# First batch of a fused cross-covariance attention and max-out feed-forward kernel: q norms as column sums on TensorE, products with the weights in landing order, third weight behind the first hidden products

## Chip, cores, metric

One core of a Trainium2 chip. The metric is the device time of one execution in microseconds. Kernel before: 574.05 us (three runs, 574.01 to 574.26). In lines and tables PE is TensorE (PEld its weight loads), DVE VectorE, ACT ScalarE, POOL GpSimd and SP SyncE. To evacuate is to copy a result from PSUM to SBUF.

## The reference

```python
qn = q / (norm(q, axis=1) + 1e-06)           # q, k, v: 4 x 6144 x 256; norms over the 6144 tokens
kn = k / (norm(k, axis=1) + 1e-06)
s  = kn.T @ qn / tau                          # 256 x 256 for each batch
a  = softmax(s, axis=-1)
x  = v @ a
h  = max(x @ w1, x @ w2, x @ w3)              # d_ff 768
out = h @ w_out
```

Because a is only 256 x 256, the kernel multiplies it into the weights first (the "A^T W products": the tiles `ew_ps`, evacuated to `aw`), so that each chunk of 512 tokens costs 36 products of 128x512 (`h_ps`) and 24 of 128x256 (`o_ps`). The 768 columns of each weight are taken in slices of 256. Warming products are products whose results nobody uses; they fill TensorE's wait for the softmax.

## The kernel before

The parts that matter (cuts marked):

```python
    def gram(b):
        ...                                             # kk: the k norms, while k is arriving
        for tp in range(NG // 2):                       # 24 steps, while q is arriving
            for j in range(CC):
                PE.matmul(ps[j][:, 0:C], lhsT=qt[:, tsl, jsl], rhs=kt[:, tsl, :], ...)          # Gram
                PE.matmul(ps[j][:, C:C + P], lhsT=qt[:, tsl, jsl], rhs=qt[:, tsl, jsl], ...)    # q by q: its diagonal is |q|^2
        ...
    def softmax_t(ps, rkb):
        for j in range(CC):
            DVE.tensor_tensor_reduce(out=scr, in0=ps[j][:, C:C + P], in1=ident, ..., accum_out=n2q[:, j:j + 1])
        ACT.activation(out=lnq, in_=n2q, func=AF.Ln)
        ACT.activation(out=rq, in_=lnq, func=AF.Exp, scale=-0.5, bias=neg_ln_tau)
        return exp_t(scaled([ps[j][:, 0:C] for j in range(CC)], rkb), rq)      # et: the softmax, two halves j

    def aw_first(et, aw):                               # first 256 columns of the three weights
        products(0, (0, 1)); sums(0); sums(1)
        DVE.reciprocal(out=rinv, in_=rs_ps[:, 0:CC])
        products(1, (0, 1))
        for j in range(CC):
            products(j, (2,))
        ...                                             # six evacuations, ACT and DVE in turn

    first = gram(0); six warming products; softmax_t; v_transpose_pe(0); aw_first
    v_transpose(1); hold_loads(1)                       # a guard: waits for the second V's transpose
    POOL.dma_start(out=wo_sb, in_=moe_w_out...)         # the output weight
    load_v(2); load_v(3)
    ...                                                 # then 48 chunks: h blocks and output products
```

## Time and profile before

| what | value | where it is read |
|---|---|---|
| time | 574.05 us | median of three runs |
| TensorE busy | 553.9 us, 97% of a 572.1 us span | page, part 1 |
| last piece of q in | 33.63 us | end of the wait for q in the chain |
| first h product | 37.52 us | timeline |
| products with the second slice of the weights start (end of the first h block) | 38.81 us | timeline |
| output products start | 50.63 us | timeline |

The prediction, quoted below, shows the page's chain. Here is the stretch after the last piece of q, from the timeline of the kernel before (columns: start, duration, engine, line, operation, count, and in brackets the idle time ahead of it with what ended it):

```profile
34.87 0.20 ACT L286 ACTIVATE lnq<-n2q 128x2 f32<-128x2 f32 x1 [6.00 <-DVE n2q L282]
35.34 0.91 ACT L275 ACTIVATE et<-e_in,rq 128x256 bf16<-128x256 f32 x2
36.47 0.60 ACT L377 ACTIVATE vt_sb<-vt_ps 128x512 bf16<-128x512 bf16 x1 [0.23 <-DVE vt_sb L376]
36.70 0.17 DVE L341 RECIPROCAL rinv<-rs_ps 128x2 f32<-128x2 f32 x1 [0.27 <-PE rs_ps L329]
36.97 1.21 ACT L347 ACTIVATE aw_sb<-ew_ps,rinv 128x256 bf16<-128x256 f32 x3
36.98 1.27 DVE L349 TENSOR_SCALAR aw_sb<-ew_ps,rinv 128x256 bf16<-128x256 f32 x3
37.49 0.12 PEld L389 LDWEIGHTS <-aw_sb 128*128 128x128 bf16 x2 [0.21 <-ACT aw_sb L347]
38.81 0.38 PE L311 MATMUL ew_ps<-w_sb,et 128*128 128x256 bf16 x2
```

Read it as a relay: the norms (Ln at 34.87), the softmax (35.34), the reciprocal of its row sums (36.70), the evacuations on two engines (36.97), the first h weights (37.49), and the next slice of weights at 38.81. The line at 36.47 is ScalarE's copy of its half of the transposed V.

### The profile page before, as it was taken

What the parts mean: (1) busy time and instruction counts of PE and PEld (TensorE: products, weight loads), DVE (VectorE), ACT (ScalarE), POOL (GpSimd) and SP (SyncE); (2) the same over time, 40 slices, a digit from 0 to 9 for tenths busy, and PEclk for the clock granted to TensorE, in tenths of its full rate; (3) what the DMA queues carried; (4) which work ended last, traced back from release to release, by engine and by line L of the source; (5) the groups of instructions that cost most, each with busy time, mean ns of one, the idle gap of its engine ahead of it and who ended that gap; (6) DMA issues with size and microseconds to landing.
All of it is one profiled execution on the core that took longest, in us unless ns stands there. A gap on an engine that the chain in (4) does not pass through costs nothing.

```text
span 572.1 us, 9442 instructions
## 1 busy us (share of the span) xinstructions
PE 553.9 (97%) x3349; PEld 330.7 (58%) x3350; DVE 411.1 (72%) x647; ACT 309.1 (54%) x539; POOL 235.1 (41%) x240
## 2 busy tenths in 40 slices
PE   3799999999999999999999999999999999999997
PEld 2665555555755555555575555555575555555566
DVE  0048777877577777777768777777868778778775
ACT  1044567677454576776545467767645444444443
POOL 2443357776730078776560048777750000000000
PEclk9999999999999999999999999999999999999999
DMA  9998998884598168984179339885437323132112
GB/s 143 106 146 129 136 237 126 159 135 116 99 107 160 56 107 158 134 148 110 57 128 151 99 81 140 148 141 98 124 86 154 75 75 109 56 103 64 56 55 76
DMA packets 76960, 65.64 MB, mean 115 GB/s; under 512 B 52464, under 2 KB 62576, under 8 KB 76784
## 3 DMA queue, kind: packets, MB, share of 16 engines
q0 software_dynamic: 19072, 26.48, 38.7%
q1 hardware_dynamic: 57696, 38.41, 23.7%
q8 instruction: 26, 0.43, 0.3%
q14 instruction: 22, 0.18, 0.1%
q10 hardware_dynamic: 144, 0.13, 0.1%
HBM read 78.64 MB, written 25.17 MB: 181 GB/s over the span
## 4 chain that ended last, share of the span: by engine, by line
PE 93%; DMA 5%; POOL 0%; issue 0%; DVE 0%; POOLq 0%
PE h_ps L389 65%; PE o_ps L409 22%; DMA q_sb<-in_q_dram 5%; PE gram L260 3%; PE ew_ps L311 3%; POOL k_sb L99 0%; PE o_ps L434 0%; PE ew_ps L335 0%; PE warm_ps L469 0%; PE vt_ps L372 0%; PE gram L177 0%; PE n_ps L215 0%; DVE ht_sb L395 0%; DVE o_sb L461 0%; PE n_ps L217 0%
## 5 line engine op out<-in xcount | busy, mean ns | idle before, releaser
L389 PE MATMUL h_ps<-vt_sb,aw_sb 128*128 128x512 bf16 (+1 forms) x1764 | 406.7, 375 | 0.1
L389 PEld LDWEIGHTS <-aw_sb 128*128 128x128 bf16 x1764 | 171.8, 98 | 161.3 <-DVE aw_sb L317 2.0
L394 DVE TENSOR_TENSOR s_mx<-h_ps,s_mx 128x512 bf16<-128x512 f32 (+1 forms) x294 | 198.7, 676 | 87.1 <-ACT s_mx L393 86.8
L393 ACT ACTIVATE s_mx<-h_ps 128x512 bf16<-128x512 f32 (+1 forms) x294 | 172.4, 587 | 124.9 <-PE h_ps L389 124.0
L395 DVE TENSOR_TENSOR ht_sb<-h_ps,s_mx 128x512 bf16<-128x512 f32 (+1 forms) x294 | 200.2, 681 | 31.4 <-PE o_ps L409 0.5
L203 POOL TENSOR_TENSOR acc<-acc,sq 128x768 f32<-128x768 f32 x90 | 147.6, 1651 | 70.5 <-ACT sq L197 61.6
L409 PE MATMUL o_ps<-wo_sb,ht_sb 128*128 128x256 bf16 x1128 | 153.9, 273 | 0.0
L409 PEld LDWEIGHTS <-ht_sb 128*128 128x128 bf16 x1128 | 110.4, 98 | 52.0
L412 ACT ACTIVATE o_sb<-o_ps 128x512 f32<-128x512 f32 x94 | 56.1, 597 | 85.3 <-PE o_ps L409 85.3
L110 POOL DMA_DIRECT2D v_sb<-in_v_dram x48 | 27.5, 578 | 37.7 <-DMA vt_sb<-v_sb 35.5
L197 ACT ACTIVATE sq<-q_sb 128x768 bf16<-128x768 fp8e4 x48 | 40.5, 845 | 0.0
L197 ACT ACTIVATE sq<-k_sb 128x768 bf16<-128x768 fp8e4 x48 | 40.1, 835 | 0.0
L200 POOL CAST acc<-sq 128x768 f32<-128x768 bf16 x6 | 4.9, 823 | 68.7 <-ACT sq L197 68.7
L102 POOL DMA_DIRECT2D q_sb<-in_q_dram x33 | 18.4, 564 | 5.1 <-DMA v_sb<-in_v_dram 4.1
L165 PE MATMUL kk<-k_sb 128*128 128x256 fp8e4 x48 | 7.5, 338 | 11.9 <-DVE k_sb L151 6.3
L99 POOL DMA_DIRECT2D k_sb<-in_k_dram x29 | 16.1, 555 | 3.1 <-DMA v_sb<-in_v_dram 1.2
L260 PE MATMUL gram<-k_sb,q_sb 128*128 128x512 fp8e4 x144 | 16.8, 277 | 0.0
L260 PEld LDWEIGHTS <-q_sb 128*128 128x256 fp8e4 x144 | 15.9, 136 | 0.6
L314 ACT ACTIVATE aw_sb<-ew_ps,rinv 128x384 bf16<-128x384 f32 (+1 forms) x24 | 13.2, 555 | 5.5 <-PE ew_ps L311 4.7
L311 PE MATMUL ew_ps<-w_sb,et 128*128 128x384 bf16 (+1 forms) x96 | 15.6, 313 | 0.0
L177 PE MATMUL gram<-k_sb,q_sb 128*128 128x512 fp8e4 x48 | 11.4, 332 | 2.6 <-DMA q_sb<-in_q_dram 2.4
L165 PEld LDWEIGHTS <-k_sb 128*128 128x256 fp8e4 x48 | 6.4, 182 | 12.9 <-DMA k_sb<-in_k_dram 6.6
(67 smaller groups left out, 112.9 us busy)
## 6 DMA issues: line engine op xcount, KB each, us to landing
out_dram<-o_sb SPq DMA_DIRECT2D x41, 512.0 KB, 2.9
v_sb<-in_v_dram POOLq DMA_DIRECT2D x48, 256.0 KB, 4.2
k_sb<-in_k_dram POOLq DMA_DIRECT2D x24, 192.0 KB, 6.0
q_sb<-in_q_dram POOLq DMA_DIRECT2D x24, 192.0 KB, 7.6
out_dram<-o_sb SPq DMA_DIRECT2D x13, 256.0 KB, 2.0
k_sb<-in_k_dram POOLq DMA_DIRECT2D x5, 256.0 KB, 10.8
w_sb<-in_moe_w_dram POOLq DMA_DIRECT2D x9, 128.0 KB, 5.7
kf<-in_k_dram SPq DMA_DIRECT2D x1, 1024.0 KB, 4.8
```

Of the source, the lines that this page charges most:

```text
L102: POOL.dma_start(out=qk[b][0][:, g0:g0 + w, :], in_=q_r[b][:, g0:g0 + w, :])
L110: POOL.dma_start(out=t, in_=v_r[gi // NCH, gi % NCH])
L197: ACT.activation(out=sq, in_=src, func=AF.Square)
L203: POOL.tensor_tensor(out=acc, in0=acc, in1=sq, op=ALU.add)
L260: PE.matmul(g[:, j * C:(j + 1) * C], lhsT=qt[:, tsl, j * P:(j + 1) * P], rhs=kt[:, tsl, :], start=(tp == 0 and j == 0), stop=(tp == NG // ...
L311: PE.matmul(ew[:, :w], lhsT=et[:, j, ic * P:(ic + 1) * P], rhs=w_sb[m][:, j, fsl], start=(j == 0), stop=(j == CC - 1))
L389: PE.matmul(t.rearrange("p (t n) -> p t n", n=P), lhsT=aw[m][:, ic, fsl], rhs=vt[:, tsl, ic, :], start=(ic == 0), stop=(ic == CC - 1))
L393: ACT.activation(out=s_mx, in_=hp[0], func=AF.Copy)
L394: DVE.tensor_tensor(out=s_mx, in0=hp[1], in1=s_mx, op=ALU.max)
L395: DVE.tensor_tensor(out=ht, in0=hp[2], in1=s_mx, op=ALU.max)
L409: PE.matmul(st["ps"][:, half], lhsT=ht[:, fc, t * P:(t + 1) * P], rhs=wo_sb[:, fc, :], start=(fc == 0), stop=(fc == FC - 1))
L412: ACT.activation(out=st["o"][:, t - 1:t + 1, :].rearrange("p t d -> p (t d)"), in_=st["ps"], func=AF.Copy)
```

## The change

The intent: norms that need no DVE reduction behind the last piece of q; softmax row sums ahead of the products; and an h block that can start before the third weight has landed. The core of the diff (cut where marked):

```diff
-            for j in range(CC):
-                PE.matmul(ps[j][:, 0:C], ...)
-                PE.matmul(ps[j][:, C:C + P], lhsT=qt[:, tsl, jsl], rhs=qt[:, tsl, jsl], ...)
+        def squares(g0, w):                            # half of each piece of q on each engine
+            ACT.activation(out=a[:, 0:h, :], in_=ra, func=AF.Square)
+            DVE.tensor_tensor(out=d[:, 0:h, :], in0=rd, in1=rd, op=ALU.mult)
+        def columns(rows, first=False, last=False):    # |q|^2: squares by a column of ones
+            ... PE.matmul(nq[:, j:j + 1], lhsT=t[:, r, j * P:(j + 1) * P], rhs=ones_c, ...)
+        for i, w in enumerate(QW):                     # 8 8 8 8 4 4 4 2 2 groups
+            if rows:
+                columns(rows, first=(i == 1))          # of the piece before
+            ...                                        # Gram of this piece
+            rows = squares(g0, w)
+        columns(rows, last=True)
...
-        products(0, (0, 1))
+        weight(0)
         sums(0)
+        products(0, 0)
         sums(1)
         DVE.reciprocal(out=rinv, in_=rs_ps[:, 0:CC])
-        products(1, (0, 1))
+        products(1, 0)
+        weight(1)
         for j in range(CC):
-            products(j, (2,))
-        ...                                            # six evacuations in turn
+            products(j, 1)
+        for m in range(2):
+            evacuate(CC * m, ACT)
+            evacuate(CC * m + 1, DVE)
+        def third():                                   # called in the first h block, behind its first two products
+            weight(2)
+            for j in range(CC):
+                products(j, 2)
+            for ic in range(CC):
+                evacuate(2 * CC + ic, DVE)
...
+            if m == 0 and behind_first:
+                behind_first()
...
-    for i in range(6):
+    for i in range(2):                                 # warming products
```

The PE transposes of the first V are also split over two PSUM banks (six to DVE, two to ACT, instead of four and four).

More of the change, by code (lines that the diff above doesn't have):

```diff
@@ L75 @@
     sq_pool = ctx.enter_context(tc.tile_pool(name="sq", bufs=4))
+    sqq_pool = ctx.enter_context(tc.tile_pool(name="sqq", bufs=3))
     sm = ctx.enter_context(tc.tile_pool(name="sm", bufs=2))
@@ L118 @@
     SP.dma_start(out=kf, in_=k_r[0][:, 0:HEAD, :])
-    for load, widths in ((load_k, [8] * 5), (load_q, [8] * 4 + [4, 4, 4, 2, 2])):
+    QW = [8] * 4 + [4, 4, 4, 2, 2]
+    for load, widths in ((load_k, [8] * 5), (load_q, QW)):
         g0 = HEAD if load is load_k else 0
@@ L154, with gram_first @@
     neg_ln_tau = -math.log(float(tau)) if float(tau) != 1.0 else 0.0
-    def gram(b):
-        qt, kt = qk[b]
+    def gram_first():
+        qt, kt = qk[0]
         kk = htile("kk")
@@ L170, in gram @@
             DVE.tensor_tensor(out=dkm[:, jsl], in0=kk[:, jsl], in1=ident, op=ALU.mult)
-        ps = [xtile(f"gram{j}") for j in range(CC)]
-        for tp in range(NG // 2):
-            tsl = slice(2 * tp, 2 * tp + 2)
-            last = tp == NG // 2 - 1
-            for j in range(CC):
-                jsl = slice(j * P, (j + 1) * P)
-                PE.matmul(ps[j][:, 0:C], lhsT=qt[:, tsl, jsl], rhs=kt[:, tsl, :],
-                          start=(tp == 0), stop=last, perf_mode=DR, skip_group_check=True)
-                PE.matmul(ps[j][:, C:C + P], lhsT=qt[:, tsl, jsl], rhs=qt[:, tsl, jsl],
-                          start=False, stop=last, perf_mode=DR, skip_group_check=True)
-            if tp == 11:
+        g = xtile("gram")
+        nq = htile("nq")
+        def squares(g0, w):
+            h = w // 2
+            a = sqq_pool.tile([P, QW[0] // 2, C], BF16, name="sqa")
+            d = sqq_pool.tile([P, QW[0] // 2, C], BF16, name="sqd")
+            ra, rd = qt[:, g0:g0 + h, :], qt[:, g0 + h:g0 + w, :]
+            ACT.activation(out=a[:, 0:h, :], in_=ra, func=AF.Square)
+            DVE.tensor_tensor(out=d[:, 0:h, :], in0=rd, in1=rd, op=ALU.mult)
+            return [(t, r) for t in (a, d) for r in range(h)]
+        def columns(rows, first=False, last=False):
+            for n, (t, r) in enumerate(rows):
+                for j in range(CC):
+                    PE.matmul(nq[:, j:j + 1], lhsT=t[:, r, j * P:(j + 1) * P], rhs=ones_c,
+                              start=(first and n == 0 and j == 0), stop=(last and n == len(rows) - 1),
+                              skip_group_check=True)
+        g0 = 0
+        rows = None
+        for i, w in enumerate(QW):
+            if rows:
+                columns(rows, first=(i == 1))
+            for tp in range(g0 // 2, (g0 + w) // 2):
+                tsl = slice(2 * tp, 2 * tp + 2)
+                for j in range(CC):
+                    PE.matmul(g[:, j * C:(j + 1) * C], lhsT=qt[:, tsl, j * P:(j + 1) * P], rhs=kt[:, tsl, :],
+                              start=(tp == 0 and j == 0), stop=(tp == NG // 2 - 1), perf_mode=DR,
+                              skip_group_check=True)
+            rows = squares(g0, w)
+            g0 += w
+            if i == 2:
                 kb_ps = htile("kb_ps")
@@ L187, in gram @@
                 ACT.activation(out=rkb, in_=lnk, func=AF.Exp, scale=-0.5)
-        return ps, rkb
+        columns(rows, last=True)
+        return [g[:, j * C:(j + 1) * C] for j in range(CC)], rkb, nq[:, 0:CC]
     SQW = 3
@@ L276, in exp_t, with softmax_first @@
         return et
-    def softmax_t(ps, rkb):
-        n2q = sm.tile([P, CC], FP32, name="n2q")
-        scr = sm.tile([P, P], FP32, name="scr")
-        for j in range(CC):
-            DVE.tensor_tensor_reduce(out=scr, in0=ps[j][:, C:C + P], in1=ident, scale=1.0, scalar=0.0,
-                                     op0=ALU.mult, op1=ALU.add, accum_out=n2q[:, j:j + 1])
+    def softmax_first(gs, rkb, n2q):
         lnq = sm.tile([P, CC], FP32, name="lnq")
@@ L287, in softmax_t @@
         ACT.activation(out=rq, in_=lnq, func=AF.Exp, scale=-0.5, bias=neg_ln_tau)
-        return exp_t(scaled([ps[j][:, 0:C] for j in range(CC)], rkb), rq)
+        return exp_t(scaled(gs, rkb), rq)
     def alloc_aw():
@@ L324, in aw_first, with weight @@
         rs_ps = xtile("rs_ps")
-        parts = [(m, ic, htile("ew_ps")) for m in range(3) for ic in range(CC)]
+        parts = []
+        def weight(m):
+            parts.extend((m, ic, htile("ew_ps")) for ic in range(CC))
         def sums(j):
@@ L330, in sums, with products, evacuate @@
                           start=(ic == 0 and j == 0), stop=(j == CC - 1), skip_group_check=True)
-        def products(j, ms):
+        def products(j, of):
             for m, ic, ew in parts:
-                if m in ms:
+                if m == of:
                     PE.matmul(ew[:, :FT], lhsT=et[:, j, ic * P:(ic + 1) * P], rhs=w_sb[m][:, j, 0:FT],
                               start=(j == 0), stop=(j == CC - 1))
-        products(0, (0, 1))
+        def evacuate(n, engine):
+            m, ic, ew = parts[n]
+            dst, src, r = aw[m][:, ic, 0:FT], ew[:, :FT], rinv[:, ic:ic + 1]
+            if engine is ACT:
+                ACT.activation(out=dst, in_=src, func=AF.Copy, scale=r)
+            else:
+                DVE.tensor_scalar_mul(out=dst, in0=src, scalar1=r)
+        weight(0)
         sums(0)
+        products(0, 0)
         sums(1)
         DVE.reciprocal(out=rinv, in_=rs_ps[:, 0:CC])
-        products(1, (0, 1))
+        products(1, 0)
+        weight(1)
         for j in range(CC):
-            products(j, (2,))
-        for n, (m, ic, ew) in enumerate(parts):
-            if n % 2 == 0:
-                ACT.activation(out=aw[m][:, ic, 0:FT], in_=ew[:, :FT], func=AF.Copy, scale=rinv[:, ic:ic + 1])
-            else:
-                DVE.tensor_scalar_mul(out=aw[m][:, ic, 0:FT], in0=ew[:, :FT], scalar1=rinv[:, ic:ic + 1])
-        return rinv
+            products(j, 1)
[4 more added lines that the diff above has]
+            weight(2)
+            for j in range(CC):
+                products(j, 2)
+            for ic in range(CC):
+                evacuate(2 * CC + ic, DVE)
+        return rinv, third
     vts = {}
@@ L369, in v_transpose_pe, with h_block @@
         vt = vt_tile(gi)
-        vt_ps = xtile("vt_ps", cols=TPC * C, dtype=BF16)
-        for i in range(TPC * CC):
-            PE.matmul(vt_ps[:, i * P:(i + 1) * P], lhsT=v_sb[:, i * P:(i + 1) * P], rhs=ident,
-                      is_transpose=True, start=(i == 0), stop=(i == CC * TPC - 1))
-        half = TPC * CC // 2
-        ps = vt_ps.rearrange("p (i n) -> p i n", n=P)
-        DVE.tensor_copy(out=vt[:, half:, :], in_=ps[:, half:, :])
-        ACT.activation(out=vt[:, :half, :], in_=ps[:, :half, :], func=AF.Copy)
-    def h_block(gi, aw, fc, tsl=slice(0, TPC)):
+        n = TPC * CC
+        cut = 6
+        banks = [xtile("vt_ps", cols=TPC * C, dtype=BF16), ps_h.tile([P, TPC * C], BF16, tag="h", name="vt_ps2")]
+        for b, (lo, hi) in enumerate(((0, cut), (cut, n))):
+            for i in range(lo, hi):
+                PE.matmul(banks[b][:, i * P:(i + 1) * P], lhsT=v_sb[:, i * P:(i + 1) * P], rhs=ident,
+                          is_transpose=True, start=(i == lo), stop=(i == hi - 1))
+        pa, pb = (t.rearrange("p (i n) -> p i n", n=P) for t in banks)
+        DVE.tensor_copy(out=vt[:, 0:cut, :], in_=pa[:, 0:cut, :])
+        ACT.activation(out=vt[:, cut:n, :], in_=pb[:, cut:n, :], func=AF.Copy)
+    def h_block(gi, aw, fc, tsl=slice(0, TPC), behind_first=None):
         vt = vts[gi]
@@ L463, in last_chunk @@
         SP.dma_start(out=dst[:, HT + 1, :], in_=o_sb[:, HT + 1, :])
-    ps = gram(0)
+    first = gram_first()
     warm_ps = htile("warm_ps")
-    for i in range(6):
-        PE.matmul(warm_ps, lhsT=ident, rhs=warm, start=(i == 0), stop=(i == 5))
-    et = softmax_t(*ps)
+    for i in range(2):
+        PE.matmul(warm_ps, lhsT=ident, rhs=warm, start=(i == 0), stop=(i == 1))
+    et = softmax_first(*first)
     v_transpose_pe(0)
     aw = alloc_aw()
-    rinv = aw_first(et, aw)
+    rinv, third = aw_first(et, aw)
     v_transpose(1)
@@ L537 @@
             for fc in range(FC):
-                h_block(gi, aw, fc)
+                h_block(gi, aw, fc, behind_first=third if gi == 0 and fc == 0 else None)
                 for f in gaps[fc]:
```

## The prediction

> **What bounds the kernel now.** I read the page's chain of work first, then the time-ordered chain, then the engines' timelines from 33 to 51 us, where the change acts. The page says what the end of the kernel hangs on:
>
> ```profile
> span 572.1 us, 9442 instructions
> ...
> PE 553.9 (97%) x3349; PEld 330.7 (58%) x3350; DVE 411.1 (72%) x647; ACT 309.1 (54%) x539; POOL 235.1 (41%) x240
> ...
> PE 93%; DMA 5%; POOL 0%; issue 0%; DVE 0%; POOLq 0%
> PE h_ps L389 65%; PE o_ps L409 22%; DMA q_sb<-in_q_dram 5%; PE gram L260 3%; PE ew_ps L311 3%; POOL k_sb L99 0%; PE o_ps L434 0%; PE ew_ps L335 0%; PE warm_ps L469 0%; PE vt_ps L372 0%; PE gram L177 0%; PE n_ps L215 0%; DVE ht_sb L395 0%; DVE o_sb L461 0%; PE n_ps L217 0%
> ```
>
> 93% of the span is TensorE work without a break; the 5% are the load of q. The change touches only the first batch's Gram product, softmax, and first h block. Of that, the part before 33.6 us is set by the arrival of q, and from 37.5 us on the chain is TensorE again:
>
> ```profile
> 20.91 12.72 DMA q_sb<-in_q_dram
> ...
> 34.29 1.24 PE warm_ps L469 x5
> 35.53 0.45 PE vt_ps L372 x8
> 35.98 0.61 PE ew_ps L335 x4
> 36.59 0.08 PE rs_ps L329 x4
> 36.67 0.89 PE ew_ps L335 x8
> 37.56 1.41 PE h_ps L389 x6
> 38.97 1.31 PE ew_ps L311 x12
> 40.28 2.66 PE h_ps L389 x12
> ```
>
> So there is a handover of 3.9 us between the last piece of q (33.63) and the first h product (37.52). Its only useless work is the 1.24 us of warming products, and it is cover for the softmax running on DVE and ACT. The first h block then takes 1.29 us (37.52 to 38.81), six products at 0.215, no stall. Everything the change can win is in these 3.9 us: 0.7% of the span.
>
> **What the Trainium skill says.** "TensorE: Matmul & The Clock Gate", part 1 (The HAM clock gate): the array runs at half pace until a window of about 3.4 us was busy. The trace agrees: a Gram pair (128x512 plus 128x256 in) repeats every 0.32 us from 20.67 to 25.85 and every 0.17 us from 26.17 on; the kk products, busy 1.25 us in every 2.5, never warmed it in 14 us. "ScalarE: Activation LUTs", What ACT_TABLE_LOAD costs: 186 ns + 0.833 ns per element with immediate scale and bias; a 768-wide square gives 826 ns, the trace has 845 and 835. "VectorE: DVE Perf Modes", the errata section: a plain tensor_tensor takes (N+151)/0.96 ns; 424 ns for N = 256, the trace has 417. "SBUF — State Buffer", Who interferes with whom: a DVE instruction with two SBUF inputs contends with a GpSimd instruction that reads SBUF, not with one that only writes; the trace of before has no such square on DVE, so nothing here shows it.
>
> **The change part by part.**
> *Removed.* 48 q-by-q products (219 ns each; 0.057 us of pace when warm, 0.107 cold). PE waits for q at 31.35, 32.30 and 33.67 anyway, so before the last piece this removes nothing from the path; in the last piece it saves 2 x 0.057. Also removed: two diagonal reductions on DVE (34.09 to 34.83), and four of six warming products (4 x 0.215 = 0.86 us of PE).
>
> *Added.* 9 squares on ACT and 9 on DVE and 96 one-column products. 8-group pieces cost about 1.05 us on ACT and 1.22 on DVE (the formulas above, N = 1024) against 2.5 us between pieces: hidden. Only the last piece (two groups, N = 256 each) is exposed: 33.68 + 0.42 = 34.10 on both engines. Then four one-column products; the row sums of before, the same form, took 36.32 (first weight load) to 36.67, so 0.35: norms at 34.5 us. Ln then starts near 34.53; before it started at 34.87 behind the reductions. Gain 0.34 us, and the rest follows unchanged (Ln to Exp 0.23, Exp to the first softmax half 0.24): softmax 35.00 to 35.91 instead of 35.34 to 36.25. The Gram half (e_in, 34.28 + 0.42) is ready before 35.00.
>
> *Moved, first part.* The row sums of each half now stand ahead of the products with W of that half, so the reciprocal no longer waits for four products: evacuation starts 0.62 us after the softmax instead of 0.72. It starts at 36.53 (36.97 before), and h at 36.53 + 0.47 + 0.05 = 37.05, 0.47 earlier than 37.52. V transposes: two warming products end at 34.85, V has landed by 35.15, eight transposes at 0.057 end by 35.6, so they don't hold this up. W lands in time: the gap between the second and third product at 36.01 and 36.21 puts the second weight at about 36.17, and the third was used at 36.96 without a wait.
>
> *Moved, second part.* After the two h products of the first weight (0.43) PE now does the four products of the third weight (0.43) and then needs both their evacuations, which are now both on DVE. From h start S: third-weight products from S+0.43; the first pair complete at S+0.43+0.21+0.27 = S+0.91; DVE evacuates at 0.48, the next 0.40 behind (three took 1.27): done at S+1.42 and S+1.82; last h product S+1.87 to S+2.09. With S = 37.05 the block ends at 39.14, against 38.81 before: **0.33 us later**. PE itself idles about 0.33 us ahead of h (second-weight products end at 36.72, the evacuation at 37.0) and 0.37 inside the block. What the norms won is spent on a serial evacuation.
>
> *Does 0.33 reach the end?* From 38.8 to 50.8 PE has no stall but 0.08 us at 40.2, so its lateness is carried. DVE is the next in line:
>
> ```profile
> 38.80:50.60 11.80, 11.80 (x67) 6.43 (x66) 11.06 (x20) 6.88 (x13) 2.11 (x4) 1.00 0.67 106
> ```
>
> (columns: stretch, length, busy us of PE, PE weight loads, DVE, ACT, POOL with their counts, granted clock, DMA share, GB/s). DVE is 94% busy. Its first maximum comes at 37.05 + 1.38 + 0.40 = 38.83 after the two evacuations, against 38.78, so DVE is nearly where it was and PE, later, waits for it no more. PE recovers the 0.08. The sum: +0.25 us, 574.3.
>
> **The rivals.**
> *A gain of about 0.5 us*: if the third evacuation overlapped better, or the norms came sooner. For it: the author meant it, 0.86 us of warming is removed. Against it, besides the sum: the output weight. Its load is issued at 45.36, behind a guard that waits for the second V's transpose, itself waiting for a saturated DMA queue; it lands 5.2 us later, at 50.56, and PE first uses it at 50.63.
>
> ```profile
> 45.13 0.18 POOL L480 COPY guard<-vt_sb 128x1 bf16<-128x1 bf16 x1 [8.00 <-DMA vt_sb<-v_sb]
> 45.36 0.83 POOL L483 DMA_DIRECT2D wo_sb<-in_moe_w_out_dram  x1
> ...
> 50.63 0.82 PE L409 MATMUL o_ps<-wo_sb,ht_sb 128*128 128x256 bf16 x6
> ```
>
> Nothing in that line of loads depends on PE, so a PE that comes 0.5 us earlier would wait there instead: all but 0.1 us of a gain is lost, 573.9 to 574.0. Only if the landing were earlier than this figure says would 573.5 be reached.
> *The array goes cold.* Without the q-by-q products PE does 8 Gram products (1.7 us cold) and 16 one-column products per 2.5 us. If the latter do not count as activity, it may stay at half pace; the Gram then falls behind the load and the handover runs at half speed, some 2 to 6 us lost, 576 to 580. For it: kk never warmed the array at 50%. Against it: issue is unbroken while PE is behind, and the warming products were cut on purpose. About one in ten.
> *DVE squares delay DMA descriptors.* They start just when q lands, which is when POOL issues the next load. Against it: descriptor generation need not read SBUF, and the requests run ten microseconds ahead of their landing. Worth 0 to 0.5 us.
> *DVE becomes the bound* to 51 us: one evacuation more, but early, where DVE waited 0.53 us for ACT at 38.25. Worth 0 to 0.2 us.
>
> **Range and chances.** The sum says 574.3; I allow some weight to a small gain and take 574.2. The loads cap the gain near 574.0, and a better overlap with an earlier landing reaches 573.6; a partly cold array gives the upper end, 575.4. 2% is 11.5 us, three times the whole handover; for slower that needs a cold array twice as bad as estimated. Within 2%: 0.985.
>
> **What would show it.** Ln of the q norms starting near 34.5; first h product near 37.05; a wait of PE for DVE (aw_sb) of 0.3 to 0.4 us before the last two h products of block one; the next weight's products starting near 39.15 instead of 38.81; 12 us without stalls after it; output products at about 50.9 with no wait for the load. Gram products that keep 0.21 us of pace after 28 us would show the cold array. I am wrong if PE enters the second weight slice before 38.8 and the output products follow earlier than 50.5.

## The result

The changed kernel took 574.35 us (four runs, 574.12 to 575.18) beside 574.03 us for the kernel before (four runs). A second set of five runs gave 574.25 beside 574.04. Ratios are the mean time of one kernel's fast runs over that of the other's of the same rounds, so they are not quite the ratio of these medians: 1.0008 (95% interval 0.9991 to 1.0026) and 1.0003 (0.9990 to 1.0015). The prediction had 574.2, and 574.3 by its sum.

The first profile of the changed kernel fell on its slowest run (575.18): there the last piece of q was in at 34.71 us instead of 33.63. This is not the change (a second profile had it at 33.70, and the kernel before has runs as slow), so I count all events from the last Gram piece, the first Gram product on q's last two groups, which waits for nothing but that load. The time-ordered chain of the second profile of the changed kernel (start, duration, what):

```profile
36.21 0.18 DVE rinv L374
...
36.49 0.50 DVE aw_sb L368
36.99 0.01 issue
37.00 0.61 PE h_ps L431 x2
37.61 0.44 PE ew_ps L359 x4
38.04 0.43 PE h_ps L431 x2
38.47 0.04 issue
38.51 0.39 PE h_ps L431
38.90 0.00 issue
38.90 0.39 PE h_ps L431
39.29 1.31 PE ew_ps L331 x12
40.60 2.59 PE h_ps L431 x12
```

and from its timeline:

```profile
34.56 0.17 ACT L306 ACTIVATE lnq<-nq 128x2 f32<-128x2 f32 x1 [0.34 <-PE nq L188]
35.00 0.91 ACT L300 ACTIVATE et<-e_in,rq 128x256 bf16<-128x256 f32 x2
37.97 0.88 DVE L368 TENSOR_SCALAR aw_sb<-ew_ps,rinv 128x256 bf16<-128x256 f32 x2 [0.57 <-PE ew_ps L359]
38.51 0.10 PEld L431 LDWEIGHTS <-aw_sb 128*128 128x128 bf16 x1 [0.53 <-DVE aw_sb L368]
38.90 0.10 PEld L431 LDWEIGHTS <-aw_sb 128*128 128x128 bf16 x1 [0.29 <-DVE aw_sb L368]
39.13 1.47 PE L331 MATMUL ew_ps<-w_sb,et 128*128 128x256 bf16 x12
```

The relay starts sooner: with q in at 33.70 (33.63 before), the softmax begins at 35.00 (35.34) and h at 37.00 (37.52). But the first block has two gaps: each of the two last h products waits for DVE to evacuate the third weight, one after the other, and the second slice of the weights comes at 39.13 instead of 38.81. From there on TensorE is unbroken as before (12 products of h in 2.59 us where the kernel before took 2.66).

| after the last Gram piece, us | softmax | h | second slice | output products |
|---|---|---|---|---|
| before | 1.67 | 3.85 | 5.14 | 16.96 |
| changed, both profiles | 1.26 | 3.25, 3.26 | 5.39, 5.39 | 17.14, 17.14 |

0.25 us lost at the second slice, 0.18 left at the output products, 0.2 to 0.3 us in the time.

### The profile page after: what moved, and what is told of

It is laid out like the page before. It is cut to its first block, busy times and chain, and to the rows that moved or that the text cites. A ratio compares the mean times of both kernels' runs of the same rounds, so it can differ in the third digit from the quotient of the medians.

```text
span 573.4 us, 9556 instructions
## 1 busy us (share of the span) xinstructions
PE 554.5 (97%) x3394; PEld 329.6 (57%) x3394; DVE 418.8 (73%) x653; ACT 315.3 (55%) x547; POOL 235.1 (41%) x240
## 4 chain that ended last, share of the span: by engine, by line
PE 93%; DMA 5%; POOL 0%; DVE 0%; issue 0%; ACT 0%; ACTq 0%; DVEq 0%; POOLq 0%
PE h_ps L431 65%; PE o_ps L453 21%; DMA q_sb<-in_q_dram 5%; PE gram L285 3%; PE ew_ps L331 2%; POOL k_sb L100 0%; PE o_ps L478 0%; PE ew_ps L359 0%; PE vt_ps L415 0%; DVE aw_sb L368 0%; PE warm_ps L513 0%; PE n_ps L240 0%; DVE o_sb L505 0%; DVE ht_sb L439 0%; ACT sqa L181 0%
## 5 line engine op out<-in xcount | busy, mean ns | idle before, releaser
L181 ACT ACTIVATE sqa<-q_sb 128x1024 bf16<-128x1024 fp8e4 (+2 forms) x9 | 6.9, 770 | 19.7 <-DMA q_sb<-in_q_dram 19.6
L285 PE MATMUL gram<-k_sb,q_sb 128*128 128x512 fp8e4 x144 | 16.8, 276 | 0.0
L167 PEld LDWEIGHTS <-k_sb 128*128 128x256 fp8e4 x48 | 6.4, 182 | 12.7 <-DMA k_sb<-in_k_dram 6.4
```

The source lines that it names most:

```text
L285: PE.matmul(g[:, j * C:(j + 1) * C], lhsT=qt[:, tsl, j * P:(j + 1) * P], rhs=kt[:, tsl, :], start=(tp == 0 and j == 0), stop=(tp == NG // ...
```

## The experiments

All outputs are right. Columns of the table: the same four events, from each variant's own profile; then the median of the timed runs and that of the kernel before.

| variant | softmax | h | second slice | output products | time, us | before, us |
|---|---|---|---|---|---|---|
| norms_only | 1.26 | 3.86 | 5.15 | 16.97 | 574.13 | 574.20 |
| order_only | 1.67 | 3.66 | 5.80 | 17.55 | 574.99 | 574.20 |
| third_split (array cooled) | 1.27 | 3.89 | 5.83 | 17.65 | 574.22 | 574.20 |
| third_ahead | 1.26 | 3.67 | 4.97 | 17.08 | 574.14 | 574.20 |
| wo_early_third_ahead | 1.26 | 3.68 | 4.97 | 16.79 | 574.62 | 574.06 |
| the same again (array cooled) | 1.28 | 4.31 | 5.61 | 17.43 | 573.72 | 574.04 |
| wo_early_third_split | 1.26 | 3.26 | 5.20 | 17.02 | 574.00 | 574.06 |
| wo_early_before | 1.66 | 3.85 | 5.14 | 16.96 | 574.06 | 574.06 |
| before_dve_squares | 1.66 | 3.85 | 5.14 | 16.97 | 574.11 | 574.06 |

### One half of the change at a time

norms_only: the changed Gram, norms and two warming products; the W products, V split and h block of before.

> Gram, norms and two warming products of the changed kernel; W products, V split and h block of before. Theory: softmax starts 0.4 us sooner than before, counted from the last Gram piece (1.26 for 1.67), h at 3.45, block unbroken at 1.29, second slice at 4.75; the gain of 0.4 then ends in a wait for the output weight; time 573.9 to 574.0. Rival (the squares cost more than they give, by delaying q's loads): softmax not sooner or q's landing later by several tenths against the kernels without squares, time 574.3 or more.

The softmax did come 0.41 us sooner, and none of it arrived: h at 3.86, as before (3.85). The expectation (3.45) missed a wait that the kernel before only brushes: the products with the second weight stand in front of the row sums, and that weight lands 2.5 us after the last Gram piece. From its timeline:

```profile
35.58 0.38 PE L355 MATMUL ew_ps<-w_sb,et 128*128 128x256 bf16 x2
36.25 0.38 PE L355 MATMUL ew_ps<-w_sb,et 128*128 128x256 bf16 x2 [0.29 <-DMA w_sb<-in_moe_w_dram]
36.47 0.24 PE L349 MATMUL rs_ps<-ones_c,et 128*128 128x1 bf16 x4
```

So the reordering has a reason: with sooner norms the weights' landing binds. And the squares cost nothing: time 574.13 beside 574.20.

order_only: the Gram, norms and six warming products of before; the W products, V split and h block of the changed kernel.

> Gram, norms and six warming products of before; W products, V split and h block of the changed kernel. Theory: softmax as before (1.67), h 0.1 to 0.2 sooner than before at 3.65 to 3.75, then the block takes 2.1 instead of 1.29 with 0.4 us of waiting for the evacuations: second slice at 5.8, 0.65 later than before; nothing hides that, time 574.5 to 574.7. Rival (the order is neutral): second slice within 0.2 of before and time 574.0.

As the theory had it: h 0.19 sooner, the second slice 0.66 later than before, nothing hides it, 574.99 us (ratio 1.0012, 1.0000 to 1.0024). That is 0.3 us above the range expected; the output products, 0.59 later than before, and a last Gram piece 0.10 later (33.77 against 33.67) would make up most of the 0.79 lost. The run holds the split of V's transposes as well, so its 0.19 is not that of the row sums alone (see below). The two halves do not add up, which is the point of doing both: alone the norms give 0.00 at the second slice and the order loses 0.66; together they lose 0.25, because the order lets the 0.41 us of the norms through.

### Where the loss sits: the third weight's evacuation

third_split: one evacuation of the third weight on each engine.

```diff
-                evacuate(2 * CC + ic, DVE)
+                evacuate(2 * CC + ic, ACT if ic == 0 else DVE)
```

> The changed kernel with the third weight still behind the first h pair, but its first evacuation on ScalarE and its second on VectorE. Theory: the two evacuations run side by side, the wait of 0.43 us inside the block shrinks to nearly nothing and the second slice comes at 5.15 to 5.2 (changed 5.39, before 5.14); time 574.0 to 574.1. If the serial evacuation is not what holds the block, the second slice stays at 5.35 or later and the time at 574.3.

The profile was spoilt by something that I had held for unlikely, a TensorE at half clock from 34 to 37.4 us, of which more below; its second slice (5.83) says nothing about the evacuation. The later variant wo_early_third_split has the same order in a warm run: the second slice at 5.20, inside the range expected here, and 0.19 sooner than with both evacuations on DVE. So about 0.2 us of the block's 0.4 us of waiting was the serial evacuation; the rest is the latency of a single one. The median, 574.22, lay above the expected 574.0 to 574.1.

third_ahead: the third weight's products back ahead of h, evacuations in turn on ACT and DVE.

```diff
+        weight(2)
+        for j in range(CC):
+            products(j, 2)
-        for m in range(2):
+        for m in range(3):
             evacuate(CC * m, ACT)
             evacuate(CC * m + 1, DVE)
-        def third(): ...
```

> The changed kernel with the third weight's four products put back ahead of the first h block and their two evacuations on ScalarE and VectorE in turn. Times counted from the last Gram piece (first gram of q's last two groups = 0); before: h at 3.85, second weight slice at 5.14, output products at about 17.0; changed: 3.25, 5.39, 17.1. Theory (the serial evacuation inside the block is what costs): no stall of TensorE for aw_sb inside the block, h at 3.3 to 3.4, second slice at 4.6 to 4.7, i.e. 0.7 us better than changed and 0.5 better than before. Second part of the theory (the output weight's landing caps any gain): the output products then wait for that load 0.3 to 0.5 us, and the time is 573.9 to 574.0, about 0.1 below before. Rival (no cap): no wait at the output products and 573.5. Rival (the norms are the loss, not the order): second slice still later than 5.14, time 574.3 or more.

Mostly as the theory had it. The block is unbroken, and the second slice comes 0.42 sooner than in the changed kernel and 0.17 sooner than before; not the 0.5 expected, because h itself came at 3.67: TensorE waited 0.4 us for the third weight to land:

```profile
37.16 0.33 PEld L359 LDWEIGHTS <-et 128*128 128x128 bf16 x4 [0.36 <-DMA w_sb<-in_moe_w_dram]
```

And at the output products the second part of the theory is on the chain of waits itself (its four pieces of issue, at most 0.06 us each, are left out):

```profile
36.80 5.86 DMA v_sb<-in_v_dram
42.68 2.87 DMA vt_sb<-v_sb
45.60 0.18 POOL guard L520
45.83 5.14 DMA wo_sb<-in_moe_w_out_dram
51.02 0.81 PE o_ps L449 x6
```

The chain no longer runs through TensorE: second V, its transpose, the guard, the output weight (5.14 us), output products. Without a wait for that load the way from the second slice to the output products takes 11.82 us in this order (kernel before: 16.96 less 5.14; wo_early_third_ahead, below: 16.79 less 4.97), which would have been 16.79; they came at 17.08. The 0.29 us of waiting turn a start that is 0.17 better into one that is 0.12 worse than before. It is worse, and not just no better, because the load landed later in this run: at 50.98, 17.04 after the last Gram piece, against 50.56 or 16.89 before. The median, 574.14, lay above the expected 573.9 to 574.0; one of its six runs took 576.15, without a low mean clock and without a profile.

### Lifting that cap

The output weight's load is moved up in the queue, to right behind the second V and ahead of the guard:

```diff
     load_v(1)
     wo_sb = consts.tile([P, FC, d_model], BF16, name="wo_sb")
+    POOL.dma_start(out=wo_sb, in_=moe_w_out.rearrange("(fc p) d -> p fc d", p=P))
...
     hold_loads(1)
-    POOL.dma_start(out=wo_sb, in_=moe_w_out.rearrange("(fc p) d -> p fc d", p=P))
```

> The kernel before with only that load moved up. Theory: its TensorE does not wait for the output weight (it comes 0.07 us after the landing), so nothing changes: output products at 16.96 after the last Gram piece, time as before within 0.1 us. If the landing already cost the kernel before something in its other runs, it is faster by a tenth or two.

The control: nothing changed at all (16.96, and 574.06 beside 574.06). The kernel before did not lose anything to that load.

> The variant with the third weight ahead of the first h block (second slice at 4.97 after the last Gram piece, output products at 17.08 because they wait for the output weight), with the output weight's load moved up in the queue, behind the second V and ahead of the guard. Theory (the output weight's landing takes what the start wins): no wait at the output products, they come 11.74 after the second slice, at 16.7, and the time is 573.75 to 573.9, 0.2 to 0.4 below that variant. Rival (some other transfer binds as well, or the moved load delays another one): output products still at 17.0 or later, or a new wait at the second V's transpose; time 574.1.

The wait is gone; output products at 16.79, 0.29 sooner than without the move, 0.17 sooner than before. The profiled run took 573.70. But the median of its five runs was 574.62, with single runs of 575.82, 575.37 and 574.62. The rival is not borne out by the trace, yet this kernel had to be run again.

> The variant with the third weight behind the first h pair and its evacuations on both engines, with the output weight's load moved up. Theory: with the array warm there is no wait of 0.43 inside the block, second slice at 4.95 to 5.05 (changed 5.39), output products 11.74 later, at 16.75; time 573.8 to 573.9. The last profile of this order showed the array at half pace from 34 to 37 us (warming products 0.43 apart, second slice at 5.83); if that comes with the order and not by chance, this profile shows it again and the time is 574.2 or more.

The softmax and h are as in the changed kernel, and the array stayed warm, but the second slice came at 5.20, not 4.95 to 5.05: I had reckoned with no wait in the block, and there is one of 0.2 us, since even the first evacuation (ready 1.49 us after h starts) comes later than the four h products and four W products ahead of it (1.29). Time 574.00.

### Do the squares on VectorE hold up the loads?

> The kernel before with the nine VectorE squares of q added, their results unused (outputs stay right). Rival of the prediction: squares with two SBUF inputs hold up the GpSimd engine that writes the load descriptors, so q lands later. If so, the last Gram piece comes 0.3 to 1 us later than in the kernels without squares (33.67 and 33.77; first to last piece 13.0 and 12.7) and the time grows by as much. If not, 13.0 again and the time within 0.1 us of before.

```diff
+        for w in [8] * 4 + [4, 4, 4, 2, 2]:
+            h = w // 2
+            d = sqq_pool.tile([P, 4, C], BF16, name="sqd")
+            rd = qt[:, g0 + h:g0 + w, :]
+            DVE.tensor_tensor(out=d[:, 0:h, :], in0=rd, in1=rd, op=ALU.mult)
+            g0 += w
```

No: from the first to the last piece of q 12.95 us (before 13.0, order_only 12.7), 574.11 us. That alone says little, for only one of q's loads is issued after the first square has started (21.32 against 21.06). But that issue, the next one of V and three of W each overlap a square, and took GpSimd 0.53, 0.53, 0.73, 0.71 and 0.70 us, the same as without the squares. The rival falls. The late q in the first profile of the changed kernel has another cause, and stays open: the kernel before has such runs too (575.38 and 575.41 among its 29).

### The array that cools

Two of the fourteen profiles, third_split and the second one of wo_early_third_ahead, show what the prediction had counted among the rivals, but at another place. All of these kernels come up to full pace between 24 and 29 us. In these two the pace halves again as the last piece of q arrives. Busy time by stretch for third_split (columns: stretch, length, busy us and counts of PE, PE weight loads, DVE, ACT, POOL, granted clock, DMA share, GB/s):

```profile
30.50:34.00 3.50, 3.04 (x42) 2.09 (x40) 2.17 (x4) 1.93 (x4) 2.46 (x4) 1.00 1.18 148
34.00:35.70 1.70, 1.68 (x14) 0.78 (x12) 1.18 (x3) 1.26 (x5) 1.21 (x3) 0.55 1.44 194
35.70:37.50 1.80, 1.80 (x18) 1.49 (x16) 0.75 (x3) 1.02 (x4) 1.72 (x3) 0.50 1.44 193
37.50:39.00 1.50, 1.50 (x12) 0.93 (x10) 1.02 (x3) 0.93 (x3) 0.00 (x0) 0.97 1.49 204
```

and for the second run of wo_early_third_ahead:

```profile
30.50:33.70 3.20, 2.75 (x40) 2.04 (x39) 1.87 (x4) 1.68 (x4) 2.17 (x4) 1.00 1.17 145
33.70:37.20 3.50, 3.50 (x27) 2.27 (x27) 1.95 (x6) 2.30 (x7) 3.00 (x6) 0.52 1.43 192
```

The third number from the right is the granted clock, 0.50 to 0.55 where it should be 1.00: half for 3.41 us in both by the clock records that the traces keep, over the handover, and from 6.83 us, twice that, after the array came up to pace. The column alone is not enough: it reads 1.00 from 20 to 25 us too, where eight Gram products of third_split took 1.97 us, against 1.07 once warm. The pace of the products shows both. The eight V transposes take 1.06 us instead of 0.62, and the second slice comes 0.64 us later (5.61 against 4.97). TensorE was 86 to 87% busy by the records in the 3.2 to 3.5 us ahead of it, but much of that were one-column products: many instructions, little streaming. The removed q-by-q products had streamed 128 columns each. The busy share itself tells nothing: from 30.50 to 34.00 the kernel before was busy for only 2.42 of 3.50 us and stayed warm, and wo_early_third_ahead for 3.07 in the profile that stayed warm and 3.06 in the one that cooled.

> The changed kernel again, unaltered, for more timed runs and a second profile. By the first profile it is 0.17 us behind before where the output products start (17.14 against 16.96 after the last Gram piece). Expected: that again within 0.05 if q lands at the usual 33.6 to 34.0 us, and a median 0.1 to 0.4 us above before, with single runs 0.5 us and more above when the array cools during the last pieces of q.

The changed kernel again: output products at 17.14 to the hundredth, 574.25 us, five runs from 574.01 to 575.11, none with the low mean clock (the 575.11 has another cause, not known). So cooling is not what holds the changed kernel behind; the block is.

> The same kernel as wo_early_third_ahead, to see whether its slow runs (574.62, 575.37, 575.82 beside 573.70 and 573.89) come back. If they come with the kernel, a third or more of the runs are again above 574.5; if they were chance, the median is 573.8.

The profiled run was the cooled one (574.37, mean clock 0.997); the other four took 573.57 to 573.94, the median 573.72. Of the three slow runs of the first set one (574.62) has the same mean clock of 0.997. The other two (575.82, 575.37, mean clock 1.000) had no profile: open, though a late q as in the changed kernel's first profile would fit.

To keep the array warm, the next variant puts five warming products into TensorE's waits for q:

```diff
             rows = squares(g0, w)
             g0 += w
+            for n in range((0, 0, 0, 2, 1, 1, 1, 0, 0)[i]):
+                PE.matmul(fill_ps[0], lhsT=ident, rhs=warm, start=True, stop=True)
```

> wo_early_third_ahead with the five warming products in the waits for q. If its slow runs come from an array that cools before or during the handover, they are gone and the median is 573.75, below before and below the changed kernel; if they come from elsewhere (the moved load, the DMA queue), slow runs stay.

Five runs from 573.71 to 573.94, median 573.76 beside 574.04: no slow run, and below both kernels. Ratio 0.9993 (0.9981 to 1.0006); the repeat without the fill had a median of 573.72, and five runs are few to show that slow ones are gone. Counted from the last square of q (the fill delays the last Gram piece itself a little, so the other anchor will not do), the second slice comes at 4.91, as in wo_early_third_ahead (4.91), so the fill is hidden behind the third weight's landing.

> The changed kernel with five more warming products (512 wide, results unused) in TensorE's waits between the later pieces of q, where they cost nothing. If runs of the changed kernel are slow now and then because its light load lets the array cool, the spread shrinks to 0.3 us and the median falls to 574.2; if the spread has another cause (late loads), nothing changes. The block's own wait stays: second slice at 5.39.

In the changed kernel the fill did not help: 574.17 us, 574.05 to 574.74. In its profile q's pieces came bunched, the fill stood in the way of the Gram, and the softmax started 1.63 us after the last square instead of 1.20. It tells nothing on cooling, as the changed kernel had no cooled run in nine.

Kernels with the column sums and no fill had the mean clock of 0.997 in 3 of 40 runs; kernels with the q-by-q products or the fill in none of 54. That, with the two traces, speaks for the light load as the cause; three cases do not prove it.

## Why the prediction was right

**Only the handover can change, 3.9 us.** Right. From the second slice to the output products the changed kernel needed 11.75 us and the kernel before 11.82.

**Norms 0.34 us sooner.** Right in kind, a little small: the softmax came 0.41 sooner, Ln 0.38 (0.82 us after the last Gram piece instead of 1.20). The squares took what the working said: for N = 256 0.42 us on both engines, for 1024 1.06 on ScalarE and 1.23 on VectorE (third_split), although the skill states the VectorE formula for fp32 adds only.

**Row sums ahead, h 0.47 us sooner.** It was 0.60, from the 0.41 and the order's 0.19 (order_only alone shows the 0.19; the working had 0.10, and its own terms add up to 0.44). The reason that the working gives is only half of it. The row sums no longer stand behind four products, but in the kernel before ScalarE's first evacuation, for which h waits, also follows straight on its copy of V (36.47 for 0.60, then 36.97): sooner sums alone could not have moved it. The split of V's transposes makes that copy smaller (0.36 us) and lets it start sooner. In the changed kernel, with fewer warming products, it matters less: by norms_only, where the unsplit copy starts 2.35 us after the last Gram piece, ScalarE would be free some 0.1 us later than its evacuation now starts (2.73), which is an estimate. No run has the split alone or leaves it out alone.

**W lands in time.** True of the changed kernel, but only just: the six products around the second weight took 0.85 us, in order_only 0.81. The step was read off the kernel before, and that it held was luck. In norms_only the second weight held TensorE for 0.29 us, in third_ahead the third for 0.4. The predicted time for a kernel with the norms alone would have been too low.

**The block takes 2.09 us instead of 1.29.** Measured 2.13 and 2.14. third_ahead (unbroken block) and order_only (0.66 lost) show that this is the loss. Of it 0.43 us are the moved W products, 0.2 the serial evacuation (third_split's order in a warm run), 0.2 the latency of one.

**+0.33 at the second slice, +0.25 in all.** Measured 0.25 and 0.18, because h came sooner than reckoned; 0.2 to 0.3 in the medians. The interval of the timed runs, 0.9991 to 1.0026, spans -0.5 to +1.5 us, so the sign rests on the traces. TensorE recovered its 0.07 to 0.08 us as predicted, and did not wait for DVE.

**A gain would be swallowed by the output weight.** Shown by third_ahead, and by lifting it.

**The cold array.** Half wrong: warming up was never in danger, cooling down was, 0.6 us at a time and seldom.

## What to carry to other kernels

A relay of short steps between a load and a busy engine is worth timing from the load's landing, and a part that wins inside it must be followed to the next load that the same engine will ask for: here 0.4 us of sooner norms met a weight's landing, then an evacuation, then another weight's landing, each just behind the last. Moving work behind the first consumer does not help if the moved work has an evacuation that the same block needs. And where one-column products take the place of streaming ones, look whether TensorE's pace falls back: it did in two profiles here, for 3.4 us each. That the light load is the cause is likely and not proven, and filling the waits had no slow run in five in one kernel and delayed the softmax in another.

## What the Trainium skill lacked or had wrong

- "TensorE: Matmul & The Clock Gate", part 1 and its table of goals, warns of idle gaps of more than about 3 us. In third_split the clock was halved (0.50 to 0.55 for 3.41 us) with no gap above 0.6 us in the 6 us ahead, and TensorE 87% busy by the records. The page also tells of a kernel in which short idles between groups make the clock swing, and says that transposes do not count as busy in the same way; it has no measure of how much streaming counts, and does not say whether one-column products do.
- The same page says that the activity window is free-running, so that the same kernel's onset varies. The traces agree for the fall as well: the same kernel cooled in one profile (0.52) and not in the other (wo_early_third_ahead), which costs 0.64 us when it happens. In both cooled profiles the half clock lasted 3.41 us and began 6.83 us after the rise, which fits windows of one length.
- "SBUF — State Buffer", Who interferes with whom: why a probe did not see tensor_tensor stall a DMA (it takes no part of what descriptor generation needs) is called inferred there. before_dve_squares agrees with what the probe saw: five issues of loads that overlap such squares took 0.53 to 0.73 us, each the same as without them.
- No page has how long a queued load of this kind takes from issue to landing behind others: the output weight (384 KB, cast) took 5.1 to 5.2 us with the two V loads behind it, and that decided whether a gain of 0.17 us was kept.
